# Five engine streams written into the main block instead of into blocks of their own

## The chip, the cores and the metric

The kernel runs on one core of a Trainium2 chip. The metric is the device time of one execution in microseconds (us); lower is better. The profile's "span" is the stretch from the first to the last instruction that belongs to the program; the device time is a little longer than the span, because it also holds something of what the runtime does around the program.

## The reference

The kernel computes a transformer layer whose two branches start from the same normalised input. `x` is 2048 x 512, bf16:

```
xn  = layernorm(x)
A   = sliding-window attention of xn: 32 heads of 16, each query looks at 8 keys,
      at distances 0, 2, ... 14; then the output projection wo
B   = (gelu(xn @ w_gate) * (xn @ w_up)) @ w_down        # 512 -> 1376 -> 512
out = x + A + B
```

## The kernel before, in words

The 2048 rows are worked through in four blocks of 512. For each block TensorE (PE) makes q, k and v (line 1036) and the two feed-forward products (line 1256), VectorE (DVE) multiplies q with shifted k and the probabilities with shifted v (lines 1067, 1218), ScalarE (ACT) evicts and applies the gelu (lines 1266, 1273, 1381), GpSimd (POOL) writes constants at the start and four small powers later (line 800). The last products of a tile of 128 rows add both branches in one accumulator (line 1348); DVE or ACT evict it, `x` is added (lines 1386, 1392), and SyncE (SP) issues the store (line 1399). SP also issues every load, the first ones at lines 698 and 647.

The order of the work on each engine is written out by hand in five strings (`ORDER`). `Graph.schedule` gives the tiles their buffers by it and `Graph.assign_sync` works out which semaphore each task waits for. `Graph.emit_engine(name, e)` (line 323) then writes one engine's instructions: for each task its waits (line 335), the instruction, and the semaphore that it raises. Only the `sp` stream has something behind its last task: for each of the last seven tasks, all of them stores, it waits until the data has landed (lines 344 to 346):

```
        if eng_name == "sp":
            for q in self.order["sp"][-7:]:
                e.wait_ge(q.sem, q.val)
```

So SP's stream ends only when the output is in memory, and the output depends on all that the other engines did.

Where these instructions are put is the matter of the change. `nc.Block()` is entered at line 484, as the first thing in the kernel's `ExitStack`. Five functions decorated with `block.sync`, `block.scalar`, `block.vector`, `block.gpsimd` and `block.tensor` are registered in it; each calls `G.emit_engine` for its engine. Every engine's stream goes into a block of its own, and an engine gets into its block by a branch from the main block. When the `ExitStack` is left, each engine branches to a common end block that closes the program: every engine drains and reports, GpSimd counts the reports and releases all of them. The profile gives the instructions of this end to line 483 (the `with` line).

Ahead of all this stands an opening barrier of the same kind, which belongs to the construction of the program object and carries line 1448 in the profile. It writes the constant tiles and has nothing to do with `nc.Block()`.

Of the kernel before, what the change touches and what calls it, by code (L numbers as in the profile page):

```python
# [438 lines left out]
def bass_parallel_sum__sliding_local_dilated__glu_gated_geglu__prompt_kernel(nc, A_x, A_wqkv, A_wo, B_x, B_w_gate, B_w_up, B_w_down, out, dbg=None, cfg=None):  # L439
# [41 lines left out]
    out2 = out[0]  # L481

    with contextlib.ExitStack() as es:
        block = es.enter_context(nc.Block())

        def sb(name, shape, dt):
            return es.enter_context(nc.sbuf_tensor(name, shape, dt))

# [56 lines left out]
        G = Graph()  # L545
# [867 lines left out]
        REPORT.update(G.report())  # L1413
        REPORT["graph"] = G

        @block.sync
        def _(e):
            G.emit_engine("sp", e)

        @block.scalar  # L1420
        def _(e):
            G.emit_engine("act", e)

        @block.vector
        def _(e):
            G.emit_engine("dve", e)

        @block.gpsimd
        def _(e):
            G.emit_engine("pool", e)  # L1430

        @block.tensor
        def _(e):
            G.emit_engine("pe", e)


# [26 lines left out]
```

## Time and profile before

| what | value |
|---|---|
| device time, three runs | 182.46, 182.43, 182.41 us (median 182.43) |
| span of the profiled execution | 180.3 us |
| device time less span | 2.1 us (182.43 - 180.3) |
| PE busy | 176.3 us (98%) |
| DVE, ACT, POOL busy | 168.8, 132.7, 20.0 us |
| granted TensorE clock | full over the span |

The profiled execution has no time of its own in the listing; the three runs lie within 0.05 us, so its time is taken as that of the median. The span is measured between program instructions, with those of the opening barrier (line 1448) and of the end (line 483) included. In the profile's views an engine's name with a "q" behind it (SPq, PEldq, POOLq) means an instruction of that engine's sequencer, such as a wait, a branch, a drain or the issue of a transfer; these are not counted as busy time. PEld is TensorE's weight load.

### The profile page before, as it was taken

What the parts mean: (1) busy time and instruction counts of PE and PEld (TensorE: products, weight loads), DVE (VectorE), ACT (ScalarE), POOL (GpSimd) and SP (SyncE); (2) the same over time, 40 slices, a digit from 0 to 9 for tenths busy, and PEclk for the clock granted to TensorE, in tenths of its full rate; (3) what the DMA queues carried; (4) which work ended last, traced back from release to release, by engine and by line L of the source; (5) the groups of instructions that cost most, each with busy time, mean ns of one, the idle gap of its engine ahead of it and who ended that gap; (6) DMA issues with size and microseconds to landing.
All of it is one profiled execution on the core that took longest, in us unless ns stands there. A gap on an engine that the chain in (4) does not pass through costs nothing.

```text
span 180.3 us, 2783 instructions
## 1 busy us (share of the span) xinstructions
PE 176.3 (98%) x1060; PEld 91.0 (50%) x1060; DVE 168.8 (94%) x157; ACT 132.7 (74%) x270; POOL 20.0 (11%) x23
## 2 busy tenths in 40 slices
PE   8899999999999999999999999999999999999994
PEld 2797554444544445444444454444444444447464
DVE  3799998799999999999999999999999999999962
ACT  5689999999999998999895898953277676520110
POOL 6000250000720009107000000000000000000000
PEclk9999999999999999999999999999999999999999
DMA  4997690964261400002933000352150127710023
GB/s 114 365 357 160 131 316 7 290 226 105 59 218 29 88 4 0 0 0 61 224 99 87 29 0 0 87 138 98 50 184 4 58 58 201 265 58 4 0 73 102
DMA packets 27276, 19.60 MB, mean 109 GB/s; under 512 B 13856, under 2 KB 25088, under 8 KB 27264
## 3 DMA queue, kind: packets, MB, share of 16 engines
q1 hardware_dynamic: 27264, 19.44, 37.8%
q8 instruction: 8, 0.13, 0.3%
q14 instruction: 4, 0.03, 0.1%
HBM read 14.71 MB, written 3.15 MB: 99 GB/s over the span
## 4 chain that ended last, share of the span: by engine, by line
PE 95%; DMA 2%; SPq 0%; issue 0%; DVE 0%; DVEq 0%
PE PS L1256 38%; PE PS L1348 29%; PE PS L1036 17%; PE PS L953 3%; DMA Wqkv<-in_A_wqkv_dram 2%; PE PS L1011 2%; PE PS L1295 2%; PE PS L1103 1%; PE PS L1110 1%; PE PS L967 1%; SPq L698 0%; PE PS L878 0%; DVE OB L1392 0%; PE PS L889 0%; DVEq L335 0%
## 5 line engine op out<-in xcount | busy, mean ns | idle before, releaser
L1348 PE MATMUL PS<-Wd,HT 128*128 128x512 bf16 (+2 forms) x209 | 40.4, 345 | 0.0
L1256 PE MATMUL PS<-xnT,Wu 128*128 128x512 bf16 x160 | 39.3, 379 | 0.0
L1256 PE MATMUL PS<-xnT,Wg 128*128 128x512 bf16 x160 | 39.0, 379 | 0.0
L1218 DVE TENSOR_TENSOR UNI<-VN,PT 128x8192 f16<-128x8192 bf16 x8 | 35.3, 4417 | 0.0
L1067 DVE TENSOR_TENSOR UNI<-QT,KT 128x8192 f16<-128x8192 bf16 x8 | 35.2, 4418 | 0.0
L1036 PE MATMUL PS<-xnT,Wqkv 128*128 128x512 bf16 x144 | 34.4, 379 | 0.0
L1348 PEld LDWEIGHTS PS<-Wd,HT 128*128 128x128 bf16 x209 | 19.6, 98 | 19.0
L1381 ACT ACTIVATE OB<-PS 128x512 bf16<-128x512 f32 x14 | 8.3, 593 | 24.1 <-PE PS L1348 22.4
L1266 ACT ACTIVATE GG<-PS 128x512 bf16<-128x512 f32 x40 | 23.2, 599 | 3.3 <-PE PS L1256 2.7
L1273 ACT ACTIVATE UU<-PS 128x512 bf16<-128x512 f32 x40 | 23.4, 605 | 3.0 <-PE PS L1256 1.6
L1256 PEld LDWEIGHTS PS<-xnT,Wu 128*128 128x128 bf16 x160 | 15.5, 98 | 18.9 <-ACT GG L1266 0.4
L1256 PEld LDWEIGHTS PS<-xnT,Wg 128*128 128x128 bf16 x160 | 15.6, 98 | 18.5 <-ACT UU L1273 0.4
L800 POOL TENSOR_TENSOR sq<-ve,mhalf 128x2 bf16<-128x2 f32 x4 | 17.1, 4282 | 64.1 <-ACT ve L796 64.1
L1036 PEld LDWEIGHTS PS<-xnT,Wqkv 128*128 128x128 bf16 x144 | 16.2, 113 | 15.3 <-ACT GG L1266 0.4
L1079 DVE TENSOR_TENSOR UNI<-UNI 128x8192 f16<-128x8192 f16 x4 | 17.7, 4418 | 0.1
L1227 DVE TENSOR_TENSOR UNI<-UNI 128x8192 f16<-128x8192 f16 x4 | 17.7, 4420 | 0.0
L1348 PE MATMUL PS<-Wo,OT 128*128 128x512 bf16 (+2 forms) x76 | 16.3, 345 | 0.0
L1280 DVE TENSOR_TENSOR HT<-GG,UU 128x1024 bf16<-128x1024 bf16 x20 | 13.2, 685 | 0.4 <-ACT UU L1273 0.4
L1348 PEld LDWEIGHTS PS<-Wo,OT 128*128 128x128 bf16 x76 | 7.1, 98 | 6.5 <-DVE OT L1238 0.2
L1233 DVE TENSOR_TENSOR UNI<-UNI 128x4096 f16<-128x4096 f16 x4 | 9.2, 2289 | 0.1
L1047 ACT ACTIVATE VN<-PS 128x512 bf16<-128x512 f32 x12 | 7.1, 602 | 2.0 <-PE PS L1036 1.9
L1047 ACT ACTIVATE KT<-PS 128x512 bf16<-128x512 f32 x12 | 7.1, 602 | 1.6 <-PE PS L1036 1.5
(98 smaller groups left out, 179.3 us busy)
## 6 DMA issues: line engine op xcount, KB each, us to landing
PT<-pt_scratch SPq DMA_DIRECT2D x16, 256.0 KB, 4.1
out_dram<-OB SPq DMA_DIRECT2D x14, 128.0 KB, 2.0
XIN<-in_A_x_dram SPq DMA_DIRECT2D x12, 128.0 KB, 3.9
Wqkv<-in_A_wqkv_dram SPq DMA_DIRECT2D x3, 512.0 KB, 5.1
XIN<-in_A_x_dram SPq DMA_DIRECT2D x6, 256.0 KB, 5.3
Wg<-in_B_w_gate_dram SPq DMA_DIRECT2D x2, 640.0 KB, 7.3
Wu<-in_B_w_up_dram SPq DMA_DIRECT2D x2, 640.0 KB, 6.9
Wd<-in_B_w_down_dram SPq DMA_DIRECT2D x1, 1280.0 KB, 6.6
```

The lines of the kernel that those rows point to most:

```text
L800: "pool", "sq%d" % t, 5.0, lambda e, t=t, n=n: e.tensor_tensor(out=sq[:, t:t + n], in0=ve[:, t:t + n], in1=mhalf[:, 0:n], op=ALU.pow),
L1036: ins = e.matmul(PS[:, 512 * it.slot:512 * it.slot + 512], lhsT=wcols(which, kt, g), rhs=xnT[:, itx.slot, kt, :], start=(kt == 0), stop=(k ...
L1047: return e.activation(out=o, in_=PS[:, 512 * it.slot:512 * it.slot + 512], func=ACTF.Identity, scale=(QSC, 1.0, 1.0)[which])
L1067: return lambda e: e.tensor_tensor(out=UNI[:, it.slot:it.slot + 2, :, :], in0=bass.AP(QT, (itq.slot * 4 + 2 * h) * 512, [[NQT * 4 * 512, 1 ...
L1079: return lambda e: e.tensor_tensor(out=UNI[:, i0.slot:i0.slot + 2, :, :], in0=UNI[:, i0.slot:i0.slot + 2, :, :], in1=UNI[:, i1.slot:i1.slo ...
L1218: return lambda e: e.tensor_tensor(out=bass.AP(UNI, ito.slot * 4096, [[NUNI * 4096, 128], [2048, 4], [512, 4], [1, 512]]), in0=bass.AP(VN, ...
L1227: return lambda e: e.tensor_tensor(out=UNI[:, i0.slot:i0.slot + 2, :, :], in0=UNI[:, i0.slot:i0.slot + 2, :, :], in1=UNI[:, i1.slot:i1.slo ...
L1256: ins = e.matmul(PS[0:M, 512 * it.slot:512 * it.slot + 512], lhsT=Wx[:, kt, j * 128:j * 128 + M], rhs=xnT[:, itx.slot, kt, :], start=(kt = ...
L1266: return lambda e: e.activation(out=GG[:, ito.slot, q, :], in_=PS[:, 512 * it.slot:512 * it.slot + 512], func=ACTF.Gelu_apprx_tanh)
L1273: return lambda e: e.activation(out=UU[:, ito.slot, q, :], in_=PS[:, 512 * it.slot:512 * it.slot + 512], func=ACTF.Identity)
L1280: return lambda e: e.tensor_tensor(out=HT[:, ito.slot, j - 1:j + 1, :], in0=GG[:, ig.slot, :, :], in1=UU[:, iu.slot, :, :], op=ALU.mult)
L1348: ins = e.matmul(PS[:, 512 * it.slot:512 * it.slot + CW], lhsT=(OT[:, ito.slot, q, ti * 128:(ti + 1) * 128] if kind == "o" else HT[:, ith. ...
```

## The change

The block is no longer entered. At the place where the five decorated functions stood, a loop calls `G.emit_engine` with each engine's own handle in turn, so that the five streams are written straight into the main block, behind the opening barrier. Each engine's instructions, their order and their waits are what they were, the seven waits at the end of `sp` included. No tile, transfer or semaphore of the kernel's own is changed.

```
     with contextlib.ExitStack() as es:
-        block = es.enter_context(nc.Block())
-
...
-        @block.sync
-        def _(e):
-            G.emit_engine("sp", e)
-
-        @block.scalar
-        def _(e):
-            G.emit_engine("act", e)
-
-        @block.vector
-        def _(e):
-            G.emit_engine("dve", e)
-
-        @block.gpsimd
-        def _(e):
-            G.emit_engine("pool", e)
-
-        @block.tensor
-        def _(e):
-            G.emit_engine("pe", e)
+        for name, e in (("sp", nc.sync), ("act", nc.scalar), ("dve", nc.vector), ("pool", nc.gpsimd), ("pe", nc.tensor)):
+            G.emit_engine(name, e)
```

## The prediction

> **What bounds the kernel now.** I read the page's span and busy times first, then its chain that ended last, then the span cut into stretches.
>
> ```profile
> span 180.3 us, 2783 instructions
> ...
> PE 176.3 (98%) x1060; PEld 91.0 (50%) x1060; DVE 168.8 (94%) x157; ACT 132.7 (74%) x270; POOL 20.0 (11%) x23
> ...
> PE 95%; DMA 2%; SPq 0%; issue 0%; DVE 0%; DVEq 0%
> ```
>
> ```profile
> core 0: us, PE busy (x) PEld busy (x) DVE busy (x) ACT busy (x) POOL busy (x), PEclk, DMA share, GB/s
> ...
> 140.00:176.00 36.00, 36.00 (x198) 18.47 (x197) 34.13 (x31) 14.53 (x28) 0.00 (x0) 1.00 0.30 90
> 176.00:180.40 4.40, 1.96 (x26) 1.68 (x23) 1.14 (x3) 0.17 (x1) 0.00 (x0) 1.00 0.33 103
> ```
>
> TensorE bounds the kernel: 176.3 of 180.3 us, and 95% of the chain that ended last. From 20 us to about 178 us there is no gap in it; the row for 140 to 176 us is 36.00 of 36.00. The change touches none of its matmuls, so all that can move lies at the two ends: before TensorE has its first weights, and in the last 4.4 us, where PE is busy for 1.96 us and the rest is the last addition, the last store and a closing sequence. I look at the end first. The chain of waits from 176 us on:
>
> ```profile
> 175.92 2.05 PE PS L1348 x26
> ...
> 178.06 0.29 DVE OB L1392
> ```
>
> The chain view stops at the last working instruction, the addition that ends at 178.35. Behind it come the last store and the waits for its landing. The SP timeline, the size row of that store, the answer for line 346, and the same line asked again for the window from 179.89 us on:
>
> ```profile
> 177.68 1.04 SPq L1399 DMA_DIRECT2D out_dram<-OB  x2
> ```
> ```profile
> out_dram<-OB SPq DMA_DIRECT2D x1, 32.0 KB, 1.5
> ```
> ```profile
> L346 SPq EVENT_SEMAPHORE  x3: 28/28/28, 178.8 to 179.9; - x3
> ```
> ```profile
> nothing on L346; most used: ['L483']
> ```
>
> The last store's issue ends at 178.72 (177.68 + 1.04), it lands 1.5 us after it was issued, and SP's last wait for landings is over by 179.89. The output is complete there. Seven waits stand in the source but there are only three records of 28 ns: I read them as two semaphores to a record, with the seventh on the branch that follows. What comes behind belongs to line 483, the block:
>
> ```profile
> L483 POOLq EVENT_SEMAPHORE  x2: 17/17/17, 180.1 to 180.2; - x2
> L483 POOLq DRAIN  x1: 3536/3536/3536, 81.6 to 81.6; - x1
> L483 ACTq DRAIN  x1: 607/607/607, 175.6 to 175.6; - x1
> L483 PEldq DRAIN  x1: 1355/1355/1355, 176.6 to 176.6; - x1
> L483 DVEq DRAIN  x1: 303/303/303, 178.1 to 178.1; - x1
> L483 SPq COMPARE_BRANCH  x1: 41/41/41, 179.9 to 179.9; - x1
> L483 SPq DRAIN  x1: 13/13/13, 180.1 to 180.1; - x1
> L483 SPq EVENT_SEMAPHORE  x1: 17/17/17, 180.3 to 180.3; - x1
> L483 ACTq EVENT_SEMAPHORE  x1: 17/17/17, 180.3 to 180.3; - x1
> L483 DVEq EVENT_SEMAPHORE  x1: 21/21/21, 180.3 to 180.3; - x1
> L483 PEldq EVENT_SEMAPHORE  x1: 51/51/51, 180.3 to 180.3; - x1
> ```
>
> The reader is to see three things. Four engines drained and were done long before SP: POOL at 85.1 (81.6 + 3.5), ACT at 176.2, PE at 178.0, DVE at 178.4. SP is the one that everybody waits for. And of all branches that the change is said to remove, the trace has a single one, on SP, at the end; there is no record of a branch at the opening on any engine.
>
> **Part one: the branches at the opening.** The chain's first pieces are SP's:
>
> ```profile
> 0.73 0.07 issue
> 0.80 0.39 SPq L698
> 1.19 0.06 issue
> ```
>
> The opening barrier lets SP go at 0.73 and the first load is issued 0.07 us later. That is where SP's branch would stand. Between its two loads, where there is none, the step is 0.06 us. So the opening branch is worth 0.01 us by the rows; at most it is the whole 0.07, and at least nothing, for the same load has to be issued either way. SP's start is on the path that sets the end (its loads release TensorE), so what is gained here would reach the end. I take 0, since the difference of 0.01 is the resolution of the rows. The other engines' start is covered by SP: PE's first weights arrive only at 5.92 us (1.71 + 4.21), as a later piece of the chain says.
>
> ```profile
> 1.71 4.21 DMA Wqkv<-in_A_wqkv_dram
> ```
>
> The Trainium skill, page "Advanced Engine Details and Errata", section Control Flow Timing, gives about 51 ns for an unconditional branch; by that figure the opening would give 0.05 us and the total below would be 181.76 instead of 181.81. The trace doesn't bear it out here: 0.07 with the branch against 0.06 without, and no branch recorded.
>
> **Part two: the closing sequence within the span.** It is in series behind SP's last wait: the branch at 179.9, SP's drain at 180.1, POOL's two semaphore steps at 180.1 and 180.2, the release of the four engines at 180.3. All of it goes; nothing lies beside it that could take its place, since the kernel has no more work and the stores have landed. One thing replaces it: the seventh wait loses the branch that it rode on and needs an instruction of its own. Its store landed long ago, so it costs one step behind 179.89: the 0.04 us between wait and branch and a record of 28 ns (L346), so the span should end at 179.95. From 180.3 (PE's release, the last, ends at 180.32) to 179.95 is a gain of 0.37 us. Bounds: 0.43 if the last record is the one at 179.89, 0.30 if the seventh wait costs a second step.
>
> **Part three: behind the span.** The runs' median is 182.43, so 2.1 us lie outside the span, in what the runtime does. No view prints what is in it; I can only bound what the change does there. Now, five engines leave the kernel together at 180.3. After it, SP leaves at 179.95 and the others at least 1.5 us earlier (DVE, the latest, at 178.4). If the runtime has steps of its own for each engine and then joins them, today's join waits for the slowest of five that start together; after the change it waits for SP alone. How far the five differ in such steps is shown by the only place where the trace has them come out of the runtime, the opening:
>
> ```profile
> L1448 SPq DRAIN  x1: 7/7/7, 0.0 to 0.0; - x1
> L1448 DVEq DRAIN  x1: 10/10/10, 0.1 to 0.1; - x1
> L1448 ACTq DRAIN  x1: 8/8/8, 0.1 to 0.1; - x1
> L1448 PEldq DRAIN  x1: 8/8/8, 0.3 to 0.3; - x1
> L1448 POOLq DRAIN  x1: 183/183/183, 0.4 to 0.4; - x1
> ```
>
> SP is the first, DVE and ACT follow by 0.1, PE by 0.3. So the extra gain lies between 0 (SP is itself the slowest on the way out, or nothing is joined) and 0.3 us (the slowest trails SP as PE does here). A loss I can exclude down to SP's own 13 ns drain: what the block's end did for the others (the drains) they had done over 1.5 us before. I take 0.25, near the upper end, because a join waits for the last engine and the nearest row is then the last one, PE's 0.3, not the 0.1 of the middle.
>
> The Trainium skill, page "Runtime: NRT & Kernel Launch", section The ~15µs preamble/postamble breakdown, says that the runtime puts a barrier of its own behind every kernel, about 1.5 us long, and that such a barrier passes from engine to engine in hops of 44 ns, eight for the round. By an estimate from that page, four of the eight hops would be done before SP arrives if SP is the turning point: 0.18 us instead of 0.25, and a total of 181.88. The same page's two closing stages after that barrier (1.5 and 2 us) don't fit in the 2.1 us that the runs have here.
>
> **The sum.** 0 + 0.37 + 0.25 = 0.62 us; 182.43 - 0.62 = 181.81 us, 0.34% less. The bounds of the three parts together: from 0.30 (nothing outside) to 0.80 (0.07 + 0.43 + 0.30), which is 182.13 to 181.63.
>
> **The rivals.**
>
> *Only the span gets shorter.* The runtime's part is as long as it was, and SP is its slowest engine: 182.43 - 0.37 = 182.06. For it speaks that SP does the transfers' bookkeeping in this kernel, so the runtime may have more to put away on it; against it, that SP is the first out at the opening (0.0 against 0.1 to 0.3).
>
> *The runtime's part grows by what the span loses.* The time outside might not start from the last instruction but wait for something with a length of its own, counted from the last store's landing at about 179.85; or the program could get a closing barrier back when it is finished. Then the time stays between 182.3 and 182.43. For it: the 2.1 us are not shown, and 0.4 us could hide in them. Against it: a release of all engines (180.3) just ahead of it is what one would expect the runtime's part to begin from.
>
> *Slower: an instruction refill comes late.* Every engine's code lies in other places when blocks are left out. The page's queue row for instruction fetches:
>
> ```profile
> q8 instruction: 8, 0.13, 0.3%
> ```
>
> Eight packets took 0.3% of 16 engines' 180.3 us, 8.65 us, or 1.08 us each. Before, none of them stops TensorE, whose stretches are full. If the shift put one such refill where TensorE has to wait for all of it, the time would be 182.43 - 0.62 + 1.08 = 182.89. It decides the sign from a stall of 0.62 us on, and shows as slower from 0.98 on. Against it: a few instructions fewer move a refill among 2120 weight loads and matmuls by almost nothing.
>
> **How the numbers follow.** 0.2% of 182.43 is 0.36 us, about what a measurement of this kernel can tell from no change, so 182.07 is the border. I give my forecast 0.62, the span alone 0.20, the unchanged total 0.14, the late refill 0.04. The forecast's cases are all faster. The span alone lands on the border (182.06), so I split it in halves: faster 0.62 + 0.10 = 0.72, same 0.10 + 0.14 = 0.24, slower 0.04. The range reaches from the forecast's lower bound, 181.63, rounded to 181.6, to 182.2, which takes in the whole of the second case with its bound of 182.13; left out are the third and the fourth, 0.18.
>
> **What the changed profile would show.** No row with line 483 at all; the last record one or two waits of line 346 with no branch behind; a span of 179.9 to 180.0; the opening unchanged (a step of 0.07 before SP's first load); PE without a gap from 20 to 178 us; and a time that exceeds the span by about 1.86 us instead of 2.1. Part one is wrong if the first load comes clearly sooner than 0.07 behind the release; part two if line 346 ends later than 179.95 or another line closes the span; part three if time less span stays at 2.1. The prediction as a whole fails if TensorE shows a new gap, or if a barrier still ends the program.

## The result, and the profile after

The changed kernel takes 181.44 us (median of six runs, 181.31 to 181.63) against 182.44 us: 1.00 us less, a ratio of 0.9943 with an interval of 0.9932 to 0.9953. Forecast were 181.81 us and a range down to 181.6. The way was right, the size was not. One execution each of the experiments `e3` and `e6` below, the profiled one, took 481 us, with TensorE's products of 512 columns at a mean of 836 ns instead of 380 and no cause found; the times given for these two are those of their other runs, and of their traces only the end is read.

The page's first lines and chain of the changed kernel:

```profile
span 179.9 us, 2772 instructions
...
PE 176.7 (98%) x1060; PEld 91.0 (51%) x1060; DVE 168.8 (94%) x157; ACT 132.9 (74%) x270; POOL 20.0 (11%) x23
...
PE 96%; DMA 1%; ACT 1%; issue 0%; SPq 0%; DVE 0%; DVEq 0%
```

Eleven instructions are gone (2783 before), and none of them worked: the work is the same. The stretches (columns as before) and the chain from 176 us on:

```profile
140.00:176.00 36.00, 36.00 (x198) 18.47 (x196) 34.13 (x31) 14.54 (x28) 0.00 (x0) 1.00 0.29 90
176.00:180.40 4.40, 1.94 (x26) 1.66 (x23) 1.14 (x3) 0.15 (x1) 0.00 (x0) 1.00 0.33 102
```
```profile
175.90 2.05 PE PS L1346 x26
...
178.04 0.29 DVE OB L1390
```

TensorE is as full as it was, and the last addition ends at 178.33, against 178.35. The lines have moved up by two behind line 484, so 1390 is 1392 of before. The answers for lines 346 and 483 (the latter for the window from 179.8 us on), and the chain at the opening:

```profile
L346 SPq EVENT_SEMAPHORE  x4: 17/28/28, 178.7 to 179.8; - x4
```
```profile
nothing on L483; most used: ['L346']
```
```profile
0.73 0.07 issue
0.80 0.40 SPq L696
1.20 0.06 issue
```

The program ends with SP's fourth wait; nothing follows. The opening is the same to 0.01 us. So much for the span, 180.32 us before and 179.86 after in the two traces. From the landing of the last store, by the trace's record of its semaphore, to the program's end it is 0.475 us before and 0.045 after: 0.43 us, free of what the span varies by. The rest of the gain lies behind the program. The time less the span is given for every run; it varies by about 0.05 us around its mean for one kernel, while the span itself varies by some tenths from run to run:

| kernel | time (median) | time less span (mean, runs) |
|---|---|---|
| before | 182.44 | 2.1 |
| before, beside the experiments | 182.5 to 182.7 | 2.10 (19 runs of the first group) |
| changed | 181.44 | 1.49 (6 runs) |
| changed, again (`e5`) | 181.39 | 1.50 (4 runs) |

Outside the span 0.62 us went, more than inside. (0.43 and 0.62 make 1.05; the medians differ by 1.00, and the difference is within what the span varies by.)

What is there can be read from the trace's records of semaphores. The views list only what the program's instructions do, but the trace holds each change of every semaphore. Semaphore 2, which the program doesn't use, is stepped nine times right behind the program, then over 200 semaphores are reset, then it is stepped nine times again. The nine steps have a fixed pattern: five, and four back. The first five, in us from the end of the span (a minus: before it):

```
step   before   e1      e3      changed   e6      e7      e8      e12
1       0.239   0.238   0.238   -1.750   -1.777   0.187  -1.781  -1.768
2       0.273   0.272   0.272   -1.716   -1.743   0.221  -1.746   0.109
3       0.485   0.484   0.310   -1.678    0.532   0.259  -1.708   0.147
4       0.528   0.528   0.355   -1.384    0.577   0.303   0.140   0.192
5       0.552   0.552   0.378    0.125    0.600   0.326   0.164   0.215
```

Before, the fifth step came 0.552 us after the program's end; now it comes after 0.125 us, since four steps are made while SP still waits for its stores. The Trainium skill, page "Runtime: NRT & Kernel Launch", section Semaphores 0–2 are reserved, names semaphore 2 as that of the runtime's barrier between the engines; the traces agree: steps of 0.023 to 0.048 us where nobody is late, and 0.10 us at the turn when SP was not the last to come. The same page's section The ~15µs preamble/postamble breakdown gives 44 ns a hop, which lies within the former. Which engine makes which step is settled by the experiments. The last of all eighteen steps comes 2.284 us behind the program's end before and 1.440 after.

### The profile page after: what moved, and what is told of

Same layout as the page of the kernel before. It is cut to its first block, busy times and chain, and to the rows that moved or that the text cites. A ratio compares the mean times of both kernels' runs of the same rounds, so it can differ in the third digit from the quotient of the medians.

```text
span 179.9 us, 2772 instructions
## 1 busy us (share of the span) xinstructions
PE 176.7 (98%) x1060; PEld 91.0 (51%) x1060; DVE 168.8 (94%) x157; ACT 132.9 (74%) x270; POOL 20.0 (11%) x23
## 4 chain that ended last, share of the span: by engine, by line
PE 96%; DMA 1%; ACT 1%; issue 0%; SPq 0%; DVE 0%; DVEq 0%
PE PS L1254 39%; PE PS L1346 29%; PE PS L1034 17%; PE PS L951 3%; PE PS L1009 2%; PE PS L1293 2%; PE PS L1101 1%; DMA XIN<-in_A_x_dram 1%; PE PS L1108 1%; PE PS L965 1%; ACT XR L726 1%; PE PS L876 0%; SPq L696 0%; ACT xnT L909 0%; PE PS L887 0%
```

## The experiments

Theory: the closing barrier is the whole effect. Beside its own 0.4 us it lets five engines loose at once, and the runtime's join then waits for the slowest of them. Rivals: the blocks and branches cost something; all engines are equally slow, so that what is paid is the join itself; where the code lies matters.

**Barrier or blocks.** `e1` puts one barrier behind the streams in the main block; `e2` keeps the blocks and their branches, but never closes the block.

```
# e1                                        # e2
             G.emit_engine(name, e)         -block = es.enter_context(nc.Block())
+        nc.all_engine_barrier()            +block = nc.Block()
                                            +block.__enter__()
```

> The streams stay in the main block, and one barrier of all five engines is put behind them. Theory (the closing barrier is the whole effect, partly by letting the engines reach the runtime's own join early): the time is that of the kernel before, 182.44 us, with a span of 180.3 and 2.1 us outside it. Rival (blocks and branches, or where the code lies, give part of it): the time stays clearly under it, between 181.6 and 182.2.

> Five blocks and the branches into them as before, but the block is never closed, so there is no branch out and no closing barrier. Theory: 181.44 us as in the changed kernel, with a span of 179.9 and 1.5 outside. Rival (blocks and branches cost something at the opening): 0.05 to 0.5 us above that.

`e1` took 182.5 us (0.9986 of before, 0.9971 to 1.0001), 2.11 us of it outside the span; `e2` 181.37 us, 1.46 outside. The barrier alone brings back all that lies outside the span, and the blocks and the branches into them cost nothing. But neither run has the branch out of the block, which SP took behind its last wait. What it cost is seen from the last landing to the program's end, by the records:

| kernel | behind SP's last wait | last landing to end, us |
|---|---|---|
| before, `e4` | branch, barrier of five engines | 0.475, 0.488 |
| `e1`, `e14`, `e17` | barrier of five engines | 0.306, 0.305, 0.305 |
| `e3` | barrier of four engines | 0.296 |
| changed, `e2`, `e5` | nothing | 0.045, 0.045, 0.045 |

So of the 0.43 us in the span the barrier is 0.26 and the branch out 0.17: SP's drain starts 0.21 us behind the end of its last wait before, and 0.04 us in `e1`. `e1` took 0.16 us less than the kernel before beside it (182.66 us), though the interval doesn't exclude the same time. The barrier's line in `e1` has the rows that line 483 had before, but for the branch:

```profile
L1416 POOLq EVENT_SEMAPHORE  x2: 17/17/17, 180.2 to 180.3; - x2
...
L1416 SPq DRAIN  x1: 13/13/13, 180.2 to 180.2; - x1
L1416 SPq EVENT_SEMAPHORE  x1: 17/17/17, 180.3 to 180.3; - x1
...
L1416 PEldq EVENT_SEMAPHORE  x1: 51/51/51, 180.3 to 180.3; - x1
```

**Who is late.** `e3` closes with a barrier of four engines, without GpSimd:

```
+        nc.multi_engine_barrier([mybir.EngineType.SP, mybir.EngineType.Activation,
+                                 mybir.EngineType.DVE, mybir.EngineType.PE])
```

> As the first run, but the closing barrier joins SP, ACT, DVE and PE alone; GpSimd ends on its own at 85 us. Theory (GpSimd is the slowest to reach the runtime's join when all are released together, by some 0.17 us): 0.15 to 0.25 us under the first run outside the span, about 1.9 instead of 2.1. Rival (all engines take about equally long, the join's passes themselves are the cost): the part outside the span stays at 2.1.

> The kernel before, unchanged, for a second trace of its end: span 180.3, 2.1 us outside. All theories expect the same; what is looked for is whether the pauses between the runtime's steps behind the span come out as in the first trace.

`e3` has 1.93 us outside the span, 0.18 less than `e1`. The table shows it in the third step: 0.484 with GpSimd in the barrier, 0.310 without, where the steps run on evenly. `e4` repeated the steps of before to 0.03 us (the fifth at 0.552). In the trace of `e3`, which is 479.7 us long, ScalarE does the counting and releasing, and no row is GpSimd's:

```profile
L1416 ACTq EVENT_SEMAPHORE  x2: 17/17/17, 479.5 to 479.6; - x2
...
L1416 SPq EVENT_SEMAPHORE  x1: 17/17/17, 479.6 to 479.6; - x1
L1416 DVEq EVENT_SEMAPHORE  x1: 21/21/21, 479.7 to 479.7; - x1
L1416 PEldq EVENT_SEMAPHORE  x1: 51/51/51, 479.7 to 479.7; - x1
```

**Each engine's way out.** `e5` is the changed kernel again. `e6`, `e7`, `e8` and `e12` move the seven last waits to the end of another engine's stream, so that this one is last and alone:

```
-        if eng_name == "sp":
+        if eng_name == "pool":      # e6; "pe" in e7, "dve" in e8, "act" in e12
             for q in self.order["sp"][-7:]:
```

> The changed kernel itself, as the control of this group: 181.4 us, 1.48 us outside the span, against 2.1 outside for the kernel before.

> The seven last waits stand at the end of GpSimd's stream instead of SP's; SP ends after issuing its last store, all else as in the changed kernel. So GpSimd is the engine that reaches the runtime's join last. Theory (each engine has a way out of its own, and GpSimd's is about 0.5 us longer than SP's): 1.9 to 2.05 us outside the span instead of 1.48, time about 181.9. Rival (GpSimd was late only because it also released the others): 1.6 or less outside, about 181.5.

> The same with the waits at the end of TensorE's stream. Theory (TensorE's way out takes about 0.24 us against SP's 0.12, and it is the first of the runtime's chain of five, so that four steps of about 0.035 us follow behind it): 1.7 to 1.8 us outside the span, time about 181.7. Rival (which engine comes last makes no difference): 1.48 outside.

> The same with the waits at the end of VectorE's stream. Theory (way out of about 0.14 us and one step of 0.024 us behind it): 1.5 to 1.57 us outside the span, time about 181.5. Rival (any engine but SP pays what GpSimd pays): 1.9 or more.

> The seven last waits at the end of ScalarE's stream, no barrier. Theory (a way out of 0.14 to 0.25 us and three steps of 0.11 us together behind it): 1.60 to 1.73 us outside the span, between VectorE's 1.44 and TensorE's 1.76. Rival (ScalarE is like VectorE): 1.44 to 1.5.

| waits last on | time | outside the span | expected outside |
|---|---|---|---|
| SP (`e5`) | 181.39 | 1.50 | 1.48 |
| VectorE (`e8`) | 181.51 | 1.44 | 1.50 to 1.57 |
| ScalarE (`e12`) | 181.50 | 1.62 | 1.60 to 1.73 |
| TensorE (`e7`) | 181.74 | 1.76 | 1.70 to 1.80 |
| GpSimd (`e6`) | 181.92 | 2.01 | 1.90 to 2.05 |

The answers for line 346 in `e6`, `e7`, `e8` and `e12` show the waits on the other engine, and they are the last of the program there too:

```profile
L346 POOLq EVENT_SEMAPHORE  x4: 17/43/43, 470.7 to 479.3; - x4
```
```profile
L346 PEldq EVENT_SEMAPHORE  x4: 51/51/51, 178.1 to 179.9; - x4
```
```profile
L346 DVEq EVENT_SEMAPHORE  x4: 21/49/50, 178.4 to 180.2; - x4
```
```profile
L346 ACTq EVENT_SEMAPHORE  x4: 17/38/38, 178.0 to 179.8; - x4
```

In the table of steps the first number behind the span stands in step 1 for TensorE (0.187), 2 for ScalarE (0.109), 3 for GpSimd (0.532), 4 for VectorE (0.140) and 5 for SP (0.125). That is the order of the join, and each engine's own way from its last instruction to it. GpSimd needs four times as long as SP. (The trace of `e6` is 479.4 us long; in `before` GpSimd's step comes 0.57 us behind GpSimd's own last instruction.) VectorE alone missed its expectation, from below, and that led on.

**The rest: code length.** In the second nine steps, SP paused for 0.47 us before the first step back in all kernels with the barrier so far, and for 0.097 to 0.099 us in those without. `e9` and `e10` lengthen SP's stream by two and by one; `e13` gives SP a drain and a semaphore step at its end; `e14` and `e15` keep the barrier, with SP's stream two longer, or four waits moved to VectorE; `e11` moves all seven.

```
# e9 (two), e10 (one), e14 (two, with the barrier): ahead of one load on SP
+            if t.name == "ldxr3":
+                for _ in range(2):
+                    e.sem_inc(self.pad)
# e11: as e8, and the barrier of e1
# e13: behind SP's last wait
+            e.drain()
+            e.sem_inc(self.pad)
# e15: with the barrier
+        late = self.order["sp"][-7:]
+        for q in {"sp": late[4:], "dve": late[:4]}.get(eng_name, ()):
```

> The changed kernel with two semaphore increments that nobody waits for put into SP's stream ahead of the load of x's tile 3 at about 91 us, where SP has time. SP's stream is then as long as with the closing barrier, without a barrier. Theory (SP's pause of 0.47 instead of 0.10 us in the last of the runtime's passes hangs on the length of SP's code, so this part of the gain isn't the barrier's): 1.60 to 1.66 us outside the span, time about 181.55. Rival (the pause belongs to the barrier): 1.49 outside and 181.4, as in the changed kernel.

> The same with one increment. If the length of SP's code decides, this shows on which side of the step one instruction lies: 1.60 to 1.66 outside the span, or 1.49 with the step between one and two. Rival: 1.49 in both.

> Main block, closing barrier of all five engines, and the seven last waits at the end of VectorE's stream instead of SP's, which makes SP's stream four instructions shorter than with the barrier alone (2.11 us outside the span). Theory of the code's length: 1.93 to 2.0 outside. Rival (the barrier makes the pause): 2.1.

> The changed kernel with what SP did in the closing barrier put behind its last wait, a drain and one semaphore step, and no join: nobody waits for it and the other four end on their own. Theory (SP's pause in the runtime's last pass comes with two more instructions behind SP's last wait for a landing): about 0.1 us longer span and 1.60 to 1.66 us outside it. Rival (the pause needs the engines released together): 1.49 outside.

> Main block, closing barrier, and two increments that nobody waits for in SP's stream at about 91 us. If the place of SP's end in its code decides, the pause of 0.47 us may change to 0.10, and then 1.93 to 2.0 us lie outside the span; if it is the barrier behind SP's own waits, the pause stays and 2.1 us lie outside.

> Main block, closing barrier, four of the seven last waits at the end of VectorE's stream and the last three still on SP, which makes SP's stream two instructions shorter. Place in the code: pause 0.10 us and 1.93 to 2.0 us outside the span. Barrier behind SP's own waits: pause 0.47 us and 2.1 outside.

SP's length does nothing: 1.48 and 1.49 us outside in `e9` and `e10` (181.47 and 181.39 us), 1.51 in `e13` (181.71 us; from the last landing to the end it has 0.095 us instead of 0.045, and most of the rest is the span's spread), 2.10 in `e14` (182.38 us), with the pause unchanged. My theory of SP's code fell. But `e11` (1.96 outside, 182.24 us) and `e15` (1.82, 182.10 us) lost the pause with the barrier in place, and `e15` fell below what was expected. Both also lengthen VectorE's stream. `e16` and `e17` lengthen that alone, without and with the barrier, by semaphore increments that nobody waits for:

```
+            if t.name == "fin10":          # on VectorE
+                for _ in range(5):         # e16, four instructions more; e17 (two more): range(3)
+                    e.sem_inc(self.pad)
```

> The changed kernel with semaphore increments that nobody waits for ahead of VectorE's addition for tile 10 (about 174 us, where VectorE has time): VectorE's stream becomes four instructions longer, as long as in the run with the waits on VectorE (1.44 us outside) and in the last one with the barrier (1.82). Theory (what the runtime does behind its second pass hangs on the length of an engine's code): 1.35 to 1.42 us outside the span, time about 181.3, which would be the fastest. Rival (it was where the waits stood): 1.49 and 181.4.

> Main block, closing barrier, all seven waits on SP, and VectorE's stream two instructions longer than with the barrier alone, as long as in the run that moved four waits. Theory (code length of VectorE): 1.8 to 1.85 us outside the span and SP's pause gone, though SP's stream is untouched. Rival (SP's end decides the pause): pause stays at 0.47 us and 2.1 lie outside.

`e16` has 1.33 us outside the span, a little less than expected, and takes 181.23 us, the fastest of all (0.9931 of before, 0.9916 to 0.9946; the changed kernel is at 0.9943 and 0.9941). `e17` has 1.82 outside and takes 182.05 us; its pause is 0.099 us with SP's stream untouched. In both, VectorE's stream has the same length. So the length of VectorE's code moves the runtime's part by 0.16 us without the barrier and by 0.29 with it. Between equals, `e17` and `e16`, the barrier costs 0.49 us outside the span.

How it does so is not the same in both. By the number of VectorE's instructions in the trace, the kernels fall into four groups. The last column is the time of the profiled execution, less its span, less the place of the last of the eighteen steps (the profiled execution of `before` has no time of its own):

| VectorE's instructions | kernels | SP's pause, us | VectorE's step behind GpSimd's in the second nine, us | time outside less last step, us |
|---|---|---|---|---|
| 182, no barrier | changed, `e2`, `e5`, `e6`, `e7`, `e9`, `e10`, `e12`, `e13` | 0.10 | 0.04 | +0.04 to +0.06 |
| 184, barrier | before, `e1`, `e3`, `e4`, `e14` | 0.47 | 0.04 | -0.19 to -0.20 |
| 186, no barrier | `e8`, `e16` | 0.10 | 0.14 | -0.20 |
| 186, barrier | `e15`, `e17` | 0.10 | 0.12 | -0.19 to -0.20 |
| 188, barrier | `e11` | 0.10 | 0.14 | +0.03 |

So the device time isn't simply the stretch up to the last step: against that it is 0.24 us shorter in some kernels than in others. The nine steps just ahead of the program stand at the same places in all traces, to 0.002 us, so the difference is likely behind it. With the barrier, two more instructions take SP's pause away. Without it there was no pause to lose: the last step of `e16` even comes later than that of the changed kernel (1.534 and 1.440 us), and its gain is in this remainder. What the remainder is, no record here shows. `e6`, `e7` and `e12` lengthen GpSimd's, TensorE's and ScalarE's streams by four instructions and stay in the first group.

The barrier's line in `e17` has the rows of `e1`, SP's release 0.16 us behind the start of SP's drain in both by the records:

```profile
L1420 SPq DRAIN  x1: 13/13/13, 180.1 to 180.1; - x1
L1420 SPq EVENT_SEMAPHORE  x1: 17/17/17, 180.2 to 180.2; - x1
...
L1420 PEldq EVENT_SEMAPHORE  x1: 51/51/51, 180.2 to 180.2; - x1
```

So the 0.29 us that it is better than `e1` aren't in the barrier. Why VectorE's length does this is open. It was tried at few lengths, and not every one helps: the longest, `e11`, lost SP's pause as well and still had 1.96 us outside, from 1.82 to 2.06 in its runs. Its trace alone has a packet of instructions fetched behind the program, 2.00 us behind its end, and the resets of semaphores 156 to 206 run there from 1.30 to 1.59 us behind the end instead of from 0.79 to 1.10 (`before`). Instruction refills behind the program may thus be the cause, but nothing here tests it.

## Why the prediction was right or wrong

*What bounds the kernel: right.* TensorE's stretches are as full as before and nothing in the middle moved.

*Part one, the opening, 0: right.* The step before the first load is 0.07 us in both traces, and `e2`, with the branches, is as fast as the change (181.37 and 181.44 us). The 51 ns of the Trainium skill's page "Advanced Engine Details and Errata", section Control Flow Timing, aren't seen at an engine's entry here; no branch is recorded there.

*Part two, the closing sequence, 0.37: right in kind, a little small.* From the last landing to the end it was 0.43 us less (0.475 and 0.045), the bound that I gave; the branch is 0.17 of it and the barrier 0.26. The seventh wait needs no step of its own: there are four records, and the last one, at 179.8, has two semaphores on it.

*Part three, behind the span, 0.25 with a bound of 0.3: wrong.* It was 0.62 us. The step that failed is this: "How far the five differ in such steps is shown by the only place where the trace has them come out of the runtime, the opening". Coming out is not going in. At the opening the five differ by 0.3 us and GpSimd is with the first; on the way to the join GpSimd takes 0.53 us after its last instruction and SP 0.125 (`e6`, `e5`). The mechanism, a join that now waits for SP alone, was right for most of it. With the engines released together the fifth step came 0.552 us behind the span, without the barrier 0.125: that is 0.43 us. GpSimd's lateness is 0.18 of it (`e1` less `e3`), the four steps ahead of SP's 0.14 (0.238 to 0.378 in `e3`), and TensorE's step, 0.238 us behind its release against SP's 0.125, the remaining 0.11. The stretch from the fifth step of the first pass to that of the second is shorter by another 0.05 (1.145 and 1.097 us in the traces). The two come to 0.48, and with equal code on VectorE the barrier costs 0.49 (`e17` less `e16`). The remaining 0.13 is what is left of two things that go against each other: SP's pause is 0.37 us shorter, and the remainder against the last step is 0.24 us longer (-0.20 to +0.05). The change also takes the barrier's two instructions from VectorE, and each of the two moved with VectorE's length in a pair of runs with the same barrier (the pause from `e1` to `e17`, the remainder from `e5` to `e16`). That the 0.13 is due to this length and not to the barrier is not shown: no run has VectorE's stream at 184 instructions without a barrier, or at 182 with one. No step of mine had it.

*The rivals.* Only the span getting shorter: no, 2.1 fell to 1.49. The runtime's part growing by what the span loses: no. A late instruction refill: no gap on TensorE (one behind the program, as in `e11`, was no rival of mine). What I weighed from the Trainium skill's page on the runtime, 0.18 us by its hops, was smaller than the 0.25 I took and further from the 0.43 measured: it counts steps alone, which make 0.14 here, and the engines' own ways to the join make the rest.

## What to carry to other kernels

The engine that waits for the last store may end the program by itself. Closing a block behind it cost 0.43 us in the program here, 0.17 for the branch and 0.26 for the barrier, and the barrier about 0.49 more behind it, because it holds back engines that had been done for over a microsecond. Put the last wait on an engine that has a short way out and stands late in the join, here SP: between kernels with the same length of VectorE's stream, 1.33 us lie outside the span with the waits on SP (`e16`) and 1.44 with them on VectorE (`e8`). GpSimd is the worst place (2.01). When an edit touches the start or the end of a program, look at the time less the span as well as at the span: more than half of this gain was there. A gain as small as 0.16 us from the length of a stream, as in `e16`, is not one to build on.

## What was not expected of the hardware

The way from an engine's last instruction to the join differs by engine: 0.11 us on ScalarE, 0.125 on SP, 0.14 on VectorE, 0.19 on TensorE and 0.53 on GpSimd. Instructions on VectorE that do nothing, at 171 us of 179.8, made the runtime's part 0.16 to 0.29 us shorter; the cause is open. And the device time, less the span, isn't the place of the last step of the runtime's join: it is 0.20 us less in some kernels and 0.05 us more in others.
